# Ordering one chunk's squares, casts and row splits behind the expert blocks they run beside

## The chip, the cores and the metric

One core of one Trainium2 chip runs the whole program. The metric is device time in microseconds (us) from launch to end, as the median of several executions. One further execution was taken with the hardware profiler, and all rows below are of that one.

## The reference

The input is x, 8 sequences of 3584 tokens with 192 channels. First comes a causal convolution of 7 taps along each sequence (8 heads of 24 channels, the taps a softmax of `weight`). Its 28672 rows then go through a mixture of 8 experts: each row is divided by its norm, multiplied with 8 normalised expert embeddings, and sent to the one expert with the largest logit.

```python
out = np.einsum('hk,bskhg->bshg', w, x_unf)          # convolution
xn = x / (np.linalg.norm(x, axis=-1, keepdims=True) + 1e-06)
logits = xn @ en.T / tau
expert_idx = np.argmax(logits, axis=1)
h = np.maximum(x[mask] @ w1[e], 0.0)                 # 192 -> 1024
out[mask] = gate_w[mask, None] * (h @ w2[e])         # 1024 -> 192
```

## The kernel before, in words

**Chunks.** The tokens are cut into 16 chunks of 1792 rows, each laid out as 112 partitions by 16 row groups. For a chunk, `mix` (line 399) does the convolution as 8 matmuls (407) that ScalarE copies back (412), then the 16 sums of squares: three of four on ScalarE (419), one of four on VectorE (422). Both engines write the squares, of which only the sums are wanted, into one tile name, `sq`, with two buffers. `route` (442) then takes the chunk in four groups of four: VectorE multiplies a group by a power of two (451), ScalarE casts it to 16 bits into `rows` (453), and VectorE subtracts the cast from the value to get the low part, in two pieces (455, 458). I call a group's four instructions a split. Transposing DMAs on SyncE's queue (`turn`, 586) bring the split rows to TensorE, which forms the logits (490); VectorE ranks them (509 to 564); and GpSimd's indirect DMAs (593) scatter the rows, with their token numbers, into one list per expert in device memory. `rows` has two buffers, so the casts of chunk c write where the scatters of chunk c-2 read.

**Blocks.** `expert` (748) takes 512, 256 or 128 rows of one expert's list as a block. Its hidden part is 8, 4 or 2 groups of matmuls (770); each fills one PSUM bank of a ring of five. Of each group ScalarE makes the high half of the hidden values (774) and VectorE, after it, the low half (776). The out part (793) reads both halves, for 128 rows at a time, 24 matmuls each; ScalarE scales the result (798) and GpSimd scatters it to the output (800). VectorE also copies the next expert's weights (697, 700) and swaps halves of the input (737).

**Stages.** In the first 150 us the weights are prepared (`prep_weights`, 288), and the first chunks are mixed and routed. Then blocks begin, and the work of the remaining chunks (3 in part, 4 to 15 in full) is emitted beside them, until about 865 us. The rest is blocks alone.

**What sets the order.** `run` (900) emits a block step by step; a step is one hidden group with its two halves, or one 128 rows of the out part. After each step it adds what VectorE and ScalarE have free in such a step to an account (`due`, never over `CAP` = 6 us) and then emits work of chunks as long as neither account is below zero. A split is booked at 0.9 + 0.95 us of VectorE and 0.85 us of ScalarE. While the chunk work waits for something (a `_Gate`), the account fills up. This emission fixes the text of the program. The order on each engine is then chosen at build time by a list scheduler, which runs a model of the machine and gives a free engine the earliest emitted instruction that is ready in the model. SyncE's order alone is the emission's. A dependency without a semaphore, which `_dep(..., False)` writes, makes the scheduler keep two instructions of an engine in order; it costs no instruction. Three such exist already: `behind` puts convolution and logit matmuls behind the last matmul emitted, `under` puts the ranking, the weight copy and the swap behind the last low half emitted (`self.low`), and the scatters name `self.step`, the last high half or output scaling emitted.

Of the kernel before, what the change touches and what calls it, by code (L numbers as in the profile page):

```python
# [13 lines left out]
F32 = mybir.dt.float32  # L14
BF16 = mybir.dt.bfloat16
I32 = mybir.dt.int32
AF = mybir.ActivationFunctionType
ALU = mybir.AluOpType
# [7 lines left out]
D = 192  # L26
# [3 lines left out]
TP = 112  # L30
# [36 lines left out]
def _dep(tc, frm, to, sync=True):  # L67
    cls = mybir.DependencyClass.Sync if sync else mybir.DependencyClass.NoSync
    tc.add_manual_dep(
        frm, to, mybir.DependencyInfo(cls, mybir.DependencyReason.DATA),  # L70
        reason="routed rows are written before they are read",
    )


class _Moe:
# [42 lines left out]
    def ps(self, ring, shape, dt, name):  # L118
        n = 2048 // (2 if dt == F16 else 4)
        t = self.rings[ring].tile([128, n], dt, tag=ring, name=name)  # L120
        w = int(np.prod(shape[1:]))
        v = t[: shape[0], :w]
        if len(shape) == 3:
            v = v.rearrange("p (a b) -> p a b", b=shape[2])
        elif len(shape) == 4:
            v = v.rearrange("p (a b c) -> p a b c", b=shape[2], c=shape[3])
        return v


    def rsqrt(self, n2, shape, name):  # L130
# [157 lines left out]
    def prep_weights(self, e, st):  # L288
        nc = self.nc
        img = self.res[:, e * RES:(e + 1) * RES]  # L290


        st, sw = st
        sr, sv = (v.bitcast(BF16).rearrange("p (n k) -> p n k", k=2)[:, :, 1]
                  for v in (st, sw))
        acc = self.sp.tile([128, 2], F32, tag="w_acc", name="w_acc")
        for k, cols in enumerate(
                ([(sr, 128, i) for i in range(NFC)]
                 + [(sr, 64, i) for i in range(NFC, 2 * NFC)],
                 [(sv, 128, i) for i in range(NFC * D // 128)])):  # L300
            if k and e >= BEHIND:

                i = nc.scalar.activation(
                    out=img[:, W2:W2 + NFC * D], in_=sw, func=AF.Square,
                    accum_out=acc[:, k:k + 1]).ins
                _dep(self.tc, i, self.act[1].name, False)
                yield
                continue
            tr = self.ps("h", [128, 128], F32, "tr_ps")
            for n, (v, rows, i) in enumerate(cols):  # L310
                v = v[0:rows, i * 128:(i + 1) * 128]
                i = nc.tensor.matmul(out=tr, lhsT=v, rhs=v, start=(n == 0),
                                     stop=(n == len(cols) - 1)).ins
                if e >= BEHIND:
                    _dep(self.tc, i, self.turned.name, False)
            dg = self.sp.tile([128, D], F32, tag="sq", name="w_dg")[:, 0:128]
            nc.vector.scalar_tensor_tensor(
                out=dg, in0=tr, scalar=1.0, in1=self.idf, op0=ALU.mult,
                op1=ALU.mult, accum_out=acc[:, k:k + 1])
            yield  # L320
        ps = self.ps("h", [128, 2], F32, "n2_ps")
        nc.tensor.matmul(out=ps, lhsT=self.onef, rhs=acc, start=True, stop=True)
        s, si = self.pow2(ps, [128, 2], 198, "w_p")
        s1, s2 = s[:, 0:1], s[:, 1:2]
        nc.vector.tensor_tensor(out=img[:, WS:WS + 2].bitcast(F32), in0=si[:, 0:1],
                                in1=si[:, 1:2], op=ALU.mult)
        yield
        xb = img[:, 2 * F:W2]
        b = img[:, W2:WS].rearrange("p (c d) -> p c d", d=2 * D)
        s_b = sw.rearrange("p (c d) -> p c d", d=D)  # L330
        hi = [nc.scalar.activation(out=o, in_=i, func=AF.Copy, scale=m).ins
              for o, i, m in ((img[:, 0:F], st[:, 0:F], s1),
                              (xb[0:64, :], st[0:64, F:2 * F], s1[0:64]),
                              (b[:, :, 0:D], s_b, s2))]
        lo = [nc.vector.scalar_tensor_tensor(
            out=o, in0=i, scalar=m, in1=h, op0=ALU.mult, op1=ALU.subtract).ins
              for o, i, m, h in (
                  (img[:, F:2 * F], st[:, 0:F], s1, img[:, 0:F]),
                  (xb[64:128, :], st[0:64, F:2 * F], s1[0:64], xb[0:64, :]),
                  (b[:, :, D:], s_b, s2, b[:, :, 0:D]))]  # L340
        if e >= BEHIND - 1:
            for i in hi:
                _dep(self.tc, i, self.act[e >= BEHIND].name, False)
        for i in lo:
            if e >= BEHIND - 2:
                _dep(self.tc, i, self.dve[e >= BEHIND].name, False)
            elif e:
                _dep(self.tc, i, self.cut.name, False)
        yield
# [36 lines left out]
            _dep(self.tc, i, self.mm.name, False)  # L386


    def under(self, i):
        if self.gated and self.low is not None:  # L390
            _dep(self.tc, i, self.low.name, False)
# [7 lines left out]
    def mix(self, c, ring, first):  # L399
        nc, sp = self.nc, self.sp  # L400

        yield _Gate(self.asked[c] + LAND_X)
        xt = self.xts[c]
        xc = xt[0:TP]
        for h in range(H):
            ps = self.ps(ring, [TP, NT, G], F32, "conv_ps")
            i = nc.tensor.matmul(out=ps, lhsT=self.band[:, h, :],  # L407
                                 rhs=xt[:, :, h * G:(h + 1) * G],
                                 start=True, stop=True).ins
            self.behind(i)  # L410
            self.clk += STEPC
            nc.scalar.copy(out=xc[:, :, h * G:(h + 1) * G], in_=ps)  # L412
            yield 0.0, 0.46

        n2 = sp.tile([TP, NT], F32, tag="n2", name="n2")
        for t in range(NT):
            sq = sp.tile([128, D], F32, tag="sq", name="sq")[0:TP, :]
            if t % 4 < NACT:
                nc.scalar.activation(out=sq, in_=xc[:, t, :], func=AF.Square,  # L419
                                     accum_out=n2[:, t:t + 1])  # L420
            else:
                nc.vector.scalar_tensor_tensor(  # L422
                    out=sq, in0=xc[:, t, :], scalar=1.0, in1=xc[:, t, :],
                    op0=ALU.mult, op1=ALU.mult, accum_out=n2[:, t:t + 1])
            if t % 2:
                yield ((0.54, 0.0), (0.27, 0.35), (0.0, 0.7))[
                    (t % 4 < NACT) + ((t - 1) % 4 < NACT)]
        s, si = self.pow2(n2[:], [TP, NT], 195, "x_p")
        y = self.rsqrt(n2[:], [TP, NT], "x_r")
        f = sp.tile([TP, NT], F32, tag="f", name="f")  # L430
        nc.vector.tensor_tensor(out=f, in0=n2, in1=y, op=ALU.mult)
        nc.vector.scalar_tensor_tensor(out=f, in0=f, scalar=1e-6, in1=s,
                                       op0=ALU.add, op1=ALU.mult)
        nc.vector.reciprocal(out=f, in_=f)
        nc.vector.tensor_scalar(out=f, in0=f, scalar1=self.rtau[:, 0:1],
                                scalar2=None, op0=ALU.mult)

        yield 1.5, 0.0
        self.mixed[c] = xc, s, si, f


    def route(self, c, xbar):
        xTs = []
        nc, sp = self.nc, self.sp
        xc, s, si, f = self.mixed.pop(c)
        r32 = self.rows[c % 2]
        rows = r32[:].bitcast(F16)
        for g in range(0, NT, GX):
            u = slice(g, g + GX)
            sb = s[:, u].unsqueeze(2).to_broadcast([TP, GX, D])  # L450
            nc.vector.tensor_tensor(out=xc[:, u, :], in0=xc[:, u, :], in1=sb,  # L451
                                    op=ALU.mult)
            nc.scalar.copy(out=rows[:, u, 0:D], in_=xc[:, u, :])  # L453
            yield 0.9, 0.85
            nc.vector.tensor_tensor(  # L455
                out=rows[:, u, 256:384], in0=xc[:, u, 0:128],
                in1=rows[:, u, 0:128], op=ALU.subtract)
            self.cut = nc.vector.tensor_tensor(
                out=rows[:, u, 192:256], in0=xc[:, u, 128:192],
                in1=rows[:, u, 128:192], op=ALU.subtract).ins  # L460
            yield 0.95, 0.0
            if xbar and 0 < g <= 2 * GX:
                xTs.append((self.turn(rows, g - GX, GX), self.queue(TURN)))
# [7 lines left out]
        for g in range(NT // GX):  # L471
            if xbar:
                if len(xTs) == g:
                    xTs.append((self.turn(rows, g * GX, GX), self.queue(TURN)))
                xT, at = xTs[g]
                yield _Gate(at + LAND_T)
            else:
                xT = self.xtp.tile([128, GX, 3, TP], F16, tag="xT", name="xT")
                for k in range(3):
                    tp = self.ps("r", [128, GX, TP], F16, "tr_ps")  # L480
                    for a in range(GX):
                        self.turned = nc.tensor.transpose(
                            out=tp[:, a, :],
                            in_=rows[:, g * GX + a, k * 128:(k + 1) * 128],
# [3 lines left out]
            for a in range(GX):  # L488
                for k in range(3):
                    i = nc.tensor.matmul(  # L490
                        out=lg[:, g * GX + a, :], lhsT=xT[:, a, k, :],
# [13 lines left out]
        if self.gated and self.step is not None:  # L505
# [19 lines left out]
                                op=ALU.mult)  # L525
# [462 lines left out]
```

## Time and profile before

| | us |
|---|---|
| median of 3 runs | 1360.71 (1360.64 to 1365.02) |
| the profiled execution | 1354.13 |
| its span, first to last instruction | 1352.4 |
| TensorE busy, mean granted clock | 1190.4 (88%), 0.94 |
| VectorE, ScalarE, GpSimd busy | 834.7, 580.9, 544.1 |

Busy time of TensorE is that of pipelined matmuls. A granted clock of 1.00 is 2.4 GHz and one of 0.50 is 1.2 GHz. A row of waits names the engine and line that sat idle and what ended the wait; "issue" is idle time for which the profile shows no releaser.

### The profile page before, as it was taken

How to read it: one execution, taken by the hardware profiler on the slowest of the kernel's cores; microseconds unless marked ns; L12 is line 12 of the kernel's file. 1: busy time of each engine (PE TensorE's matmuls, PEld its weight loads, DVE VectorE, ACT ScalarE, POOL GpSimd, SP SyncE). 2: the span in 40 equal slices, each digit the busy share in tenths (PEclk: the TensorE clock that was granted, in tenths of full speed). 3: DMA queues.
4: the chain of work that ended last, by engine and by line, in shares of the span. 5: the costliest groups of instructions: out<-in, count | busy, mean ns of one | idle time of the engine just before them, and what ended most of it. 6: DMA issues, size and time to landing. Idle time of an engine off the chain costs nothing. (4 is left out here: it accounts for less than half of the span.)

```text
span 1352.4 us, 28951 instructions
## 1 busy us (share of the span) xinstructions
PE 1190.4 (88%) x10572; PEld 909.4 (67%) x10572; DVE 834.7 (62%) x2218; ACT 580.9 (43%) x1343; POOL 544.1 (40%) x552
## 2 busy tenths in 40 slices
PE   4673789988889998999888999689999999999998
PEld 2542578777776676867556667367767777799787
DVE  3968647677766756676576664454455565467475
ACT  3967343444534644444444633223333333333332
POOL 0064252455544546445445555652222222223232
PEclk9666788899999998999989999899999999999999
DMA  8464524446446354555457444222212122113120
GB/s 247 141 215 113 108 69 99 126 99 135 100 123 149 95 117 112 121 133 129 102 124 152 86 104 96 78 72 51 51 36 55 39 52 46 34 43 66 32 46 23
DMA packets 273952, 129.12 MB, mean 95 GB/s; under 512 B 215774, under 2 KB 264285, under 8 KB 273808
## 3 DMA queue, kind: packets, MB, share of 16 engines
q1 hardware_dynamic: 250000, 80.39, 28.0%
q0 software_dynamic: 23808, 46.87, 11.6%
q8 instruction: 83, 1.36, 0.4%
q14 instruction: 61, 0.50, 0.1%
HBM read 38.35 MB, written 47.53 MB: 64 GB/s over the span
## 5 line engine op out<-in xcount | busy, mean ns | idle before, releaser
L793 PE MATMUL o_ps<-slot,hid 128*128 128x192 f16 x5544 | 514.2, 250 | 60.3 <-issue 26.5
L793 PEld LDWEIGHTS <-hid 128*128 128x128 f16 x5544 | 464.8, 99 | 110.3 <-issue 49.8
L770 PE MATMUL h_ps<-e_xT,slot 128*128 128x256 f16 (+2 forms) x2944 | 506.4, 305 | 26.5 <-issue 15.6
L770 PEld LDWEIGHTS <-slot 128*128 128x128 f16 x3680 | 327.6, 100 | 219.5 <-issue 48.9
L800 POOL DMA_INDIRECT out_dram<-y,e_mt x231 | 258.5, 1119 | 506.9 <-ACT y L798 453.9
L776 DVE SCALAR_TENSOR_TENSOR hid<-h_ps,hid 128x512 f16<-128x512 f32 x462 | 309.6, 686 | 189.0 <-ACT hid L774 159.0
L774 ACT ACTIVATE hid<-h_ps 128x512 f16<-128x512 f32 x462 | 265.4, 598 | 220.8 <-PE h_ps L770 160.4
L593 POOL DMA_INDIRECT rows_d<-rows,di x256 | 267.9, 1046 | 225.0 <-issue 83.7
L798 ACT ACTIVATE y<-o_ps,g 128x192 f32<-128x192 f32 x231 | 95.2, 419 | 334.4 <-PE o_ps L793 255.4
L770 PE MATMUL h_ps<-e_xf,slot 128*128 128x256 f16 (+2 forms) x736 | 212.4, 304 | 1.0 <-issue 1.0
L700 DVE COPY slot<-res 128x3074 f16 x88 | 85.3, 969 | 168.7 <-PE o_ps L793 110.4
L407 PE MATMUL conv_ps<-xt,band 128*112 128x384 f32 x256 | 111.6, 544 | 19.9 <-ACT xt L412 8.6
L453 ACT CAST rows<-xt 112x768 f16<-112x768 f32 x64 | 52.9, 830 | 101.4 <-DMA rows_d<-rows,di 56.7
L412 ACT COPY xt<-conv_ps 112x384 f32<-112x384 f32 x128 | 60.0, 479 | 71.6 <-PE conv_ps L407 54.1
L697 DVE COPY slot<-res 128x3072 f16 x88 | 83.8, 952 | 0.0
L490 PEld LDWEIGHTS <-xT 128*112 128x112 f16 x768 | 57.9, 148 | 28.5 <-DMA xT<-rows 16.3
L455 DVE TENSOR_TENSOR rows<-xt,rows 112x512 f16<-112x512 f32 x64 | 44.0, 687 | 48.2 <-ACT rows L453 37.1
L490 PE MATMUL lg_ps<-ma,xT 128*112 128x16 f16 x512 | 57.2, 204 | 16.7 <-DMA xT<-rows 14.8
L407 PEld LDWEIGHTS conv_ps<-xt,band 128*112 128x112 f32 x256 | 43.2, 195 | 41.7 <-issue 17.9
L419 ACT ACTIVATE sq<-xt 112x192 f32<-112x192 f32 x192 | 67.8, 355 | 2.9 <-DVE sq L422 1.7
L451 DVE TENSOR_TENSOR xt<-xt,x_p_s 112x768 f32<-112x768 f32 x64 | 58.4, 952 | 0.2
L490 PE MATMUL lg_ps<-mb,xT 128*112 128x16 f16 x256 | 46.8, 206 | 1.5 <-ACT xT L486 1.5
(163 smaller groups left out, 531.0 us busy)
## 6 DMA issues: line engine op xcount, KB each, us to landing
xt<-in_dram SPq DMA_DIRECT2D x39, 384.0 KB
xt<-in_dram SPq DMA_DIRECT2D x3, 1440.0 KB
rows_d<-rows,di POOLq DMA_INDIRECT x256
res<-in_dram SPq DMA_DIRECT2D x5, 768.0 KB
out_dram<-y,e_mt POOLq DMA_INDIRECT x231
xT<-rows SPq DMA_TRANSPOSE x224
xt<-in_dram SPq DMA_DIRECT2D x2, 1536.0 KB
hid<-in_dram SPq DMA_DIRECT2D x3, 768.0 KB
```

Of the source, the lines that this page charges most:

```text
L407: i = nc.tensor.matmul(out=ps, lhsT=self.band[:, h, :], rhs=xt[:, :, h * G:(h + 1) * G], start=True, stop=True).ins
L419: nc.scalar.activation(out=sq, in_=xc[:, t, :], func=AF.Square, accum_out=n2[:, t:t + 1])
L490: i = nc.tensor.matmul(out=lg[:, g * GX + a, :], lhsT=xT[:, a, k, :], rhs=self.mb if k == 1 else self.ma, start=(k == 0), stop=(k == 2)).ins
L593: i = self.nc.gpsimd.indirect_dma_start(out=self.rows_d[:, :], out_offset=bass.IndirectOffsetOnAxis(ap=idx, axis=0), in_=src, in_offset=No ...
L697: self.under(nc.vector.tensor_copy(out=self.slot[:, 0:W2], in_=v).ins)
L700: self.nc.vector.tensor_copy(out=self.slot[:, W2:], in_=self.res[:, bass.ds(self.we + W2, RES - W2)])
L770: self.mm = nc.tensor.matmul(out=ps[:, c, :], lhsT=w1(o, b + c), rhs=xk[k], start=(i == 0), stop=(i == 4)).ins
L774: self.step = nc.scalar.activation(out=hh[:, b:b + m, :], in_=ps, func=AF.Relu).ins
L776: self.low = nc.vector.scalar_tensor_tensor(out=hl[:, b:b + m, :], in0=ps, scalar=0.0, in1=hh[:, b:b + m, :], op0=ALU.max, op1=ALU.subtrac ...
L793: self.mm = nc.tensor.matmul(out=o, lhsT=h[:, c, q], rhs=w2[:, c, k:k + D], start=(c + i == 0), stop=(c == NFC - 1 and i == 2)).ins
L798: self.step = nc.scalar.activation(out=y, in_=o, func=AF.Copy, scale=g[:, a:a + 1]).ins
L800: i = nc.gpsimd.indirect_dma_start(out=self.out[:, :], out_offset=bass.IndirectOffsetOnAxis(ap=mt[:, a, 0:1], axis=0), in_=y, in_offset=No ...
```

## The change

Once blocks run (`gated`), the change gives an order without a semaphore to every square, multiply, cast and split part: those of ScalarE go behind `self.step`, those of VectorE behind `self.low`, as they stand at the point of emission. The squares of VectorE, and a throw-away product of the weight preparation, no longer write `sq` but a tile of their own with one buffer, which they share by its tag with `ge` of `select`, a VectorE tile. Instructions, their sizes and the emission stay the same.

```diff
+    def waste(self, p, n):
+        return self.lp.tile([128, D], F32, tag="sl_ge", name="waste")[0:p, 0:n]
...
+    def beside(self, i, act=False):
+        at = self.step if act else self.low
+        if self.gated and at is not None:
+            _dep(self.tc, i, at.name, False)
...
             if t % 4 < NACT:
-                nc.scalar.activation(out=sq, in_=xc[:, t, :], func=AF.Square,
-                                     accum_out=n2[:, t:t + 1])
+                sq = sp.tile([128, D], F32, tag="sq", name="sq")[0:TP, :]
+                self.beside(nc.scalar.activation(
+                    out=sq, in_=xc[:, t, :], func=AF.Square,
+                    accum_out=n2[:, t:t + 1]).ins, True)
             else:
-                nc.vector.scalar_tensor_tensor(
-                    out=sq, in0=xc[:, t, :], scalar=1.0, in1=xc[:, t, :],
-                    op0=ALU.mult, op1=ALU.mult, accum_out=n2[:, t:t + 1])
+                self.beside(nc.vector.scalar_tensor_tensor(
+                    out=self.waste(TP, D), in0=xc[:, t, :], scalar=1.0,
+                    in1=xc[:, t, :], op0=ALU.mult, op1=ALU.mult,
+                    accum_out=n2[:, t:t + 1]).ins)
...
-            nc.vector.tensor_tensor(out=xc[:, u, :], in0=xc[:, u, :], in1=sb,
-                                    op=ALU.mult)
-            nc.scalar.copy(out=rows[:, u, 0:D], in_=xc[:, u, :])
+            self.beside(nc.vector.tensor_tensor(
+                out=xc[:, u, :], in0=xc[:, u, :], in1=sb, op=ALU.mult).ins)
+            self.beside(nc.scalar.copy(
+                out=rows[:, u, 0:D], in_=xc[:, u, :]).ins, True)
             yield 0.9, 0.85
-            nc.vector.tensor_tensor(
+            self.beside(nc.vector.tensor_tensor(
                 out=rows[:, u, 256:384], in0=xc[:, u, 0:128],
-                in1=rows[:, u, 0:128], op=ALU.subtract)
+                in1=rows[:, u, 0:128], op=ALU.subtract).ins)
```

The second piece of the low part (458) gets no order of its own; it is emitted right behind the first and needs the same cast.

## Rows read from the trace of the kernel before

**Rows 1.** Busy time by stretch: start:end, length, engines' busy us (instructions), PEclk, DMA, GB/s.
```profile
200.00:864.00 664.00, 603.80 (x5217) 456.06 (x5216) 442.09 (x1291) 295.28 (x754) 335.60 (x336) 0.97 0.51 115
880.00:1352.00 472.00, 455.56 (x4463) 359.73 (x4461) 258.42 (x477) 168.95 (x321) 133.91 (x124) 1.00 0.20 46
```

**Rows 2.** TensorE's waits, 200 to 864 us: who waited for whom: total, times, longest.
```profile
PE o_ps L793 <- DVE hid L776: 15.5, 19, 2.1
PE o_ps L793 <- issue: 15.0, 33, 1.2
...
PE o_ps L793 <- ACT hid L774: 7.1, 8, 2.0
PE h_ps L770 <- ACT y L798: 2.6, 2, 1.9
PE o_ps L793 <- DVE rows L458: 1.8, 1, 1.8
```

**Rows 3.** Groups of instructions by line, whole span: busy us, mean ns | idle before.
```profile
L776 DVE SCALAR_TENSOR_TENSOR hid<-h_ps,hid 128x512 f16<-128x512 f32 x462 | 309.6, 686 | 189.0 <-ACT hid L774 159.0 <-issue 26.4 <-ACT sq L419 2.0
...
L407 PE MATMUL conv_ps<-xt,band 128*112 128x384 f32 x256 | 111.6, 544 | 19.9 <-ACT xt L412 8.6 <-DMA xt<-in_dram 6.5 <-issue 2.7
...
L451 DVE TENSOR_TENSOR xt<-xt,x_p_s 112x768 f32<-112x768 f32 x64 | 58.4, 952 | 0.2
...
L453 ACT CAST rows<-xt 112x768 f16<-112x768 f32 x64 | 52.9, 830 | 101.4 <-DMA rows_d<-rows,di 56.7 <-issue 25.9 <-DVE xt L451 5.6
L455 DVE TENSOR_TENSOR rows<-xt,rows 112x512 f16<-112x512 f32 x64 | 44.0, 687 | 48.2 <-ACT rows L453 37.1 <-issue 4.3 <-DMA rows_d<-rows,di 4.1
...
L458 DVE TENSOR_TENSOR rows<-xt,rows 112x256 f16<-112x256 f32 x64 | 26.7, 417 | 0.0
```

**Rows 4.** ScalarE's and VectorE's waits, 200 to 864 us.
```profile
ACT rows L453 <- DMA rows_d<-rows,di: 56.7, 19, 7.1
...
DVE rows L455 <- ACT rows L453: 37.1, 16, 4.4
DVE sq L422 <- ACT sq L419: 23.8, 16, 6.2
```

**Rows 5.** Timeline, 381 to 389 us: start us, us, engine, line, what [idle before].
```profile
386.57 0.83 ACT L453 CAST rows<-xt 112x768 f16<-112x768 f32 x1 [5.40 <-DMA rows_d<-rows,di]
...
387.44 0.69 DVE L455 TENSOR_TENSOR rows<-xt,rows 112x512 f16<-112x512 f32 x1 [3.02 <-ACT rows L453]
...
387.96 0.50 PE L793 MATMUL o_ps<-slot,hid 128*128 128x192 f16 x4 [2.04 <-ACT hid L774]
```

**Rows 6.** Chain that ended last, 836 to 860 us: start us, us, what.
```profile
840.88 8.65 PE h_ps L770 x40
849.53 3.14 PE o_ps L793 x38
```

**Rows 7.** Timeline, 362 to 371.5 us, VectorE and TensorE.
```profile
362.06 0.69 DVE L776 SCALAR_TENSOR_TENSOR hid<-h_ps,hid 128x512 f16<-128x512 f32 x1 [0.98 <-ACT sq L419]
...
369.95 0.69 DVE L776 SCALAR_TENSOR_TENSOR hid<-h_ps,hid 128x512 f16<-128x512 f32 x1
...
370.69 1.00 PE L793 MATMUL o_ps<-slot,hid 128*128 128x192 f16 x10 [1.76 <-DVE g L785]
```

**Rows 8.** Timeline, 575.5 to 580.4 us.
```profile
576.75 2.68 DVE L451 TENSOR_TENSOR xt<-xt,x_p_s 112x768 f32<-112x768 f32 x3
...
580.18 0.42 PE L793 MATMUL o_ps<-slot,hid 128*128 128x192 f16 x3 [2.12 <-DVE hid L776]
```

**Rows 9.** Busy time by stretch, with the granted clock (columns as rows 1).
```profile
207.60:214.40 6.80, 6.05 (x41) 5.37 (x39) 5.96 (x16) 0.00 (x0) 0.25 (x1) 0.50 0.27 73
388.50:392.00 3.50, 2.88 (x16) 2.32 (x17) 3.42 (x8) 0.84 (x2) 1.32 (x1) 0.51 0.78 154
```

**Rows 10.** Timeline, 14 to 30 us, VectorE and TensorE.
```profile
25.42 0.91 PE L312 MATMUL tr_ps<-res 128*128 128x128 bf16 x12
...
26.62 0.29 DVE L317 SCALAR_TENSOR_TENSOR w_dg<-tr_ps,idf 128x128 f32<-128x128 f32 x1 [11.82 <-ACT sq L419]
```

More of the change, by code (lines that the diff above doesn't have):

```diff
@@ L315, in prep_weights @@
                     _dep(self.tc, i, self.turned.name, False)
-            dg = self.sp.tile([128, D], F32, tag="sq", name="w_dg")[:, 0:128]
             nc.vector.scalar_tensor_tensor(
-                out=dg, in0=tr, scalar=1.0, in1=self.idf, op0=ALU.mult,
+                out=self.waste(128, 128), in0=tr, scalar=1.0, in1=self.idf, op0=ALU.mult,
                 op1=ALU.mult, accum_out=acc[:, k:k + 1])
@@ L416, in mix @@
         for t in range(NT):
-            sq = sp.tile([128, D], F32, tag="sq", name="sq")[0:TP, :]
             if t % 4 < NACT:
-                nc.scalar.activation(out=sq, in_=xc[:, t, :], func=AF.Square,
-                                     accum_out=n2[:, t:t + 1])
-            else:
-                nc.vector.scalar_tensor_tensor(
-                    out=sq, in0=xc[:, t, :], scalar=1.0, in1=xc[:, t, :],
-                    op0=ALU.mult, op1=ALU.mult, accum_out=n2[:, t:t + 1])
+                sq = sp.tile([128, D], F32, tag="sq", name="sq")[0:TP, :]
+                self.beside(nc.scalar.activation(
+                    out=sq, in_=xc[:, t, :], func=AF.Square,
+                    accum_out=n2[:, t:t + 1]).ins, True)
+            else:
+                self.beside(nc.vector.scalar_tensor_tensor(
+                    out=self.waste(TP, D), in0=xc[:, t, :], scalar=1.0,
+                    in1=xc[:, t, :], op0=ALU.mult, op1=ALU.mult,
+                    accum_out=n2[:, t:t + 1]).ins)
             if t % 2:
```

## The prediction

> **What bounds the kernel now.** I read the busy time by stretch first. While blocks run alone, TensorE is busy for all but 16 of 472 us; in the stage in which chunk work runs beside blocks it is idle for 60 of 664 us, and VectorE, at 442 us, is at 67% [rows 1]. So TensorE sets the pace, and the change can touch only the 60 us, the clock, and what it adds to them. The waits of TensorE in that stage say who ended them [rows 2]: the low half 15.5, the high half 7.1, the output scaling 2.6 and a split part 1.8 us, 27.0 together. The rows marked "issue" name no releaser; I leave them as they are. I went through the gaps behind the 27 us one by one: in about 25 us of them a multiply, a cast or a split part ran on VectorE or ScalarE within 2 us ahead.
>
> Why splits stand there is seen in two places. At 386.6 us a cast of ScalarE has waited 5.4 us for a scatter of the chunk that used the same `rows` buffer; VectorE's split part waits 3.0 us for the cast, the low half stands behind that, and TensorE is idle for 2.0 us [rows 5]. Such waits of casts are 56.7 us in the stage, in 19 pieces, and those of split parts for casts 37.1 us [rows 4]. At 576.8 us three multiplies run in a row ahead of a low half, and TensorE waits 2.1 us [rows 8]. Both come from one habit: the list scheduler pulls splits forward into what its model thinks idle. I numbered the program's instructions as the code emits them and read the engines' queues against it. In the gated stage all 50 multiplies stand 1 to 21 low halves ahead of their place, and 45 of 50 casts are ahead of theirs. No square is ahead: they wait for the last convolution copy anyway.
>
> **The change, part by part.** *The squares' orders* bind nothing, since no square is ahead: 0 us, hidden by the convolutions that feed them. *The tile of its own* takes away VectorE's waits for ScalarE's squares, 23.8 us in the stage [rows 4]. In the gaps that I went through next to nothing had a square ahead and a low half as releaser, so TensorE gets nothing: 0. In the head the same sharing shows a wait of 11.8 us, which could be worth anything from 0 to 11.8; but the matmuls whose product that instruction reads ended at 26.3 us, 0.3 us before it began [rows 10], so I take 0.3, since both rows belong to the very wait. The head may also come out in another order; nothing bounds that, and I leave it at 0.
>
> *The splits' orders* are the change. They take away what pulling forward costs: up to 27.0, and I take 25. A split issues no DMA, but transposes, loads of x and scatters wait for it. SyncE keeps the order of emission, and the planner emits a chunk's logits at least 5.1 + 4.5 us of its own clock (`TURN`, `LAND_T`) after the transposes; the latest bunch below ends 8.2 us after its place, so the lead covers it. The casts come at a place where the scatters of chunk c-2 have all been emitted (`route` starts with at most 16 pending), so most of the 56.7 us goes, and with it the 37.1.
>
> What do they add? The account of the planner fills to 6 us while a chunk waits for a gate, and a split books 1.85 us, so three or four splits are then emitted at one place. An order behind the last low half is also a licence: the splits are older than the next low half, all four multiplies are ready, and the scheduler gives a free engine the oldest ready instruction. So they should run as one bunch ahead of the next low half. A split takes VectorE 0.952 + 0.687 + 0.417 = 2.06 us [rows 3], four take 8.2. ScalarE's four casts, 0.83 us each [rows 3], lie beside that; a high half behind a cast is late by less than VectorE is, and costs nothing of its own.
>
> The trace of before has no such bunch in a hidden part, so its price is bounded. From below it is 0: a stretch of 7.2 us without a low half that begins in an out part, with four hidden groups to come, costs TensorE 1.8 us [rows 7]. From above it is 0.8 of the bunch, as where three multiplies meet a TensorE that has already run out of other work: 2.12 of 2.68 us [rows 8]. Between them I count what TensorE still has to do before it needs the last held half: a hidden group takes 8.65 / 8 = 1.08 us, and the out part reaches half number 8 after 7 x 3 matmuls of 3.14 / 38 us, 1.75 us in all [rows 6]; each further half takes 0.69 us [rows 3]. With j groups still to come the price is bunch + 0.69 (j - 1) - 1.08 j - 1.75. Stepping the planner through the code gives the places of the 12 full chunks:
> - Five late in a hidden part. Chunk 8, after 7 of 8 groups: 8.2 - 1.08 - 1.75 = 5.4. Chunks 11 and 12, after 6: 5.0 each. Chunk 15, after 5: 4.6. Chunk 5, three splits (6.2) after 2 of 4 groups, where the last half is needed after 1.5 us: 3.2. Together 23.
> - Four in an out part (4, 7, 10, 14): as in [rows 7], 1.8 each, 7.
> - Two beside eight convolutions (6, 13), 0.44 us each of TensorE [rows 3], which cover them: 1. One spread over three groups (9): 1.
>
> That is 32 us; the ends I keep are 0 and 51 (the five at 0.8 x 8.2 = 6.5, the rest doubled).
>
> *The clock.* After such waits the granted clock falls to half: 6.8 us at 1.2 GHz after the wait at 205 us, 3.5 us after that at 388 us [rows 9]; two more of these lengths follow split waits, so 20.6 us at half clock lose some 8 us beside what was idle anyway. These go. After the change eight waits of 2 to 5 us would bring one each, at 1.75 to 3.4 us; I take 2, so 16. Net + 8, with ends of - 8 and + 19.
>
> Sum: - 25 + 32 + 8 - 0.3 = + 15 us on the profiled execution's 1354.1 (its span is 1352.4), so 1369. That execution lies 6.6 us under the median of the three runs, 1360.7; I add them: **1376 us**.
>
> **The rivals.** *The places of emission are good ones: faster.* The emission was paced by what each step leaves free, and five PSUM banks let TensorE run on. If low halves slip in between multiplies while a cast is awaited, or the bunches mostly fall where rows 7's price or less holds, 25 us and 8 us of clock go and some 3 to 10 come: 1361 - 23 to 30, or 1331 to 1338. For it speaks that the ranking, which is under the same kind of order, costs TensorE little now; against it, that the ranking is a chain in which each instruction waits for the one before and lets a low half through, while multiplies wait for nothing. It decides above about 2.5 us a chunk: below that the forecast turns. 0.33.
>
> *No change.* Gains and bunches cancel within 7 us, or order on an engine that is a third idle matters to nobody: about 1361. 0.13. The Trainium skill, in "Perfetto Trace Analysis" under "Identifying the Most-Contended Engine", says to find the engine with the highest occupancy and work on that one first; by that VectorE, at 67%, would not be the place and the sum would be 0. The 15.5 us of TensorE's waits on low halves [rows 2] speak against reading it so here: what is late is an instruction, not an engine.
>
> *Slower by another way.* The split rows come too late for the transposes, these hold the queue of SyncE, and TensorE meets its logit matmuls, which stand in its own queue, before the transposed rows have landed. If each of 12 chunks lost the bunch beyond the covered 6 us, 2.2 us, twice, that is some 50 us less the 33 saved: about 1380. 0.06. The forecast itself gets 0.48.
>
> **How the numbers follow.** A measurement of this kernel tells some 0.5% (6.8 us) from no change. Faster 0.33, same 0.13, slower 0.48 + 0.06 = 0.54. The forecast's own range is 1362 to 1406: from a bunch price cut by a third with half the clock term, to 51 and + 19. The 8-in-10 range must hold most of the faster case too: 1329 to 1406.
>
> **What would show each step.** Right: the 56.7 us of casts waiting for scatters nearly gone, and VectorE's waits for ScalarE's squares too; three or four multiplies between two low halves late in a hidden part, five times; TensorE's waits on the low half up from 15.5 to about 35 us, in pieces of 3 to 6; eight stretches at half clock instead of four. Wrong: low halves between the multiplies of a bunch, or pieces of TensorE idle time under 2 us there; then the faster case holds. TensorE waiting for transposed rows for more than a few us would be the third rival. A first block that starts more than 3 us earlier or later would be a step that I left at 0.

## The result, and the profile after

The changed kernel takes 1381.88 us (median of four executions, 1379.47 to 1384.68), the kernel before 1362.2 us beside it: a ratio of 1.0143, 95% interval 1.0112 to 1.0173. It is slower by 20 us, where 1376 was forecast. That agreement hides that the terms of the sum were wrong, and on the two other chips on which the changed kernel ran the sign was the opposite one. The profiled execution of the changed kernel is one of the four, 1384.68 us with a span of 1383.0; before it was 1354.13 with 1352.4. So the spans of the two traces differ by 30.6 us where the medians differ by 19.7: some 11 us of what follows lie between executions and not between the kernels. The lines of the code have moved: high half 786, low half 788, output matmul 805, multiply 462, cast 464, split parts 467 and 470, transposes 601.

From the page of the changed kernel, busy time of the engines and TensorE's granted clock in 40 slices:

```profile
PE 1208.0 (87%) x10572; PEld 921.2 (67%) x10572; DVE 839.5 (61%) x2218; ACT 581.0 (42%) x1343; POOL 538.6 (39%) x552
...
PEclk9555789897899998999989999999999999999999
```

The same 10572 matmuls kept TensorE busy for 1190.4 us before; the other 17.6 us are a lower clock. The span grew by 30.6, so idle time grew by 13.0. By releaser, that is 35 us more of "issue" less 22 of other waits: 16 less between the first block and the last routing, 8 less in the head, 2 more behind (the first block starts at 147 to 148 us in both).

Busy time by stretch of the changed kernel (columns as [rows 1]):

```profile
200.00:864.00 664.00, 590.04 (x5015) 448.28 (x5014) 432.50 (x1234) 291.19 (x741) 312.46 (x319) 0.93 0.49 111
...
880.00:1352.00 472.00, 449.62 (x4269) 346.81 (x4267) 253.19 (x511) 163.98 (x313) 144.80 (x137) 0.98 0.21 49
```

Against [rows 1], 202 matmuls fewer are done in the first stretch and its clock is 0.93 instead of 0.97. The second stretch starts with chunk work still running.

TensorE's waits in the changed kernel, 200 to 890 us (total, times, longest):

```profile
PE o_ps L805 <- issue: 35.4, 44, 2.3
PE lg_ps L502 <- issue: 13.3, 17, 2.1
PE h_ps L782 <- issue: 9.6, 17, 1.1
PE h_ps L782 <- DVE hid L788: 4.9, 2, 4.1
PE o_ps L805 <- DVE hid L788: 4.6, 8, 1.2
PE o_ps L805 <- ACT hid L786: 3.7, 3, 2.3
PE lg_ps L502 <- DMA xT<-rows: 1.9, 2, 1.0
```

and the "issue" rows of the kernel before in the same stretch:

```profile
PE h_ps L770 <- issue: 16.6, 22, 6.3
PE o_ps L793 <- issue: 15.0, 33, 1.2
```

This is the opposite of the forecast. Waits with a releaser on VectorE or ScalarE shrink, as the orders were to make them [rows 2]. What grows is "issue", idle time for which the profile shows no releaser: 58.3 us in the three rows of the changed kernel, 31.6 in the two of before.

What the casts and squares waited for is gone. Groups by line, whole span, of the changed kernel (compare [rows 3]):

```profile
L462 DVE TENSOR_TENSOR xt<-xt,x_p_s 112x768 f32<-112x768 f32 x64 | 58.0, 951 | 0.0
L464 ACT CAST rows<-xt 112x768 f16<-112x768 f32 x64 | 51.9, 832 | 8.8 <-DVE xt L462 7.2 <-issue 0.6 <-DVE rows L470 0.5
L467 DVE TENSOR_TENSOR rows<-xt,rows 112x512 f16<-112x512 f32 x64 | 43.8, 685 | 0.4
```

Casts idled 101.4 us before, 8.8 now; the first split part 48.2, now 0.4.

The bunches are there too, and of the forecast length: three times all four splits of a chunk stand between two low halves. Timeline of the changed kernel, 561 to 573.7 us:

```profile
561.94 0.69 DVE L788 SCALAR_TENSOR_TENSOR hid<-h_ps,hid 128x512 f16<-128x512 f32 x1 [0.40 <-ACT hid L786]
...
563.75 3.59 DVE L462 TENSOR_TENSOR xt<-xt,x_p_s 112x768 f32<-112x768 f32 x4
...
565.07 1.47 PE L416 MATMUL conv_ps<-xt,band 128*112 128x384 f32 x4
...
566.38 1.91 PE L782 MATMUL h_ps<-e_xT,slot 128*128 128x256 f16 x16
...
570.19 0.60 PE L782 MATMUL h_ps<-e_xT,slot 128*128 128x256 f16 x4
...
572.67 0.42 DVE L470 TENSOR_TENSOR rows<-xt,rows 112x256 f16<-112x256 f32 x1
...
573.00 0.68 DVE L788 SCALAR_TENSOR_TENSOR hid<-h_ps,hid 128x512 f16<-128x512 f32 x1
```

Between the low halves at 561.94 and 573.00 stand four multiplies and their eight split parts, 8.0 us, and TensorE does not idle at all in that time (busy for 11.06 of 11.06 us): it has outputs, convolutions and the hidden groups of the next block to do. The low half at 561.94 is the last of its block, the one at 573.00 the first of the next.

Last, the lulls, as I call stretches in which TensorE and ScalarE, and mostly VectorE, all but stop though the profile shows nothing that they wait for. Two nearly equal stretches of the changed kernel, the first in a lull, the second just ahead of it (columns as [rows 1]):

```profile
697.40:708.50 11.10, 1.88 (x10) 0.81 (x9) 0.31 (x2) 0.00 (x0) 6.54 (x7) 0.70 0.51 134
685.00:696.00 11.00, 11.00 (x69) 5.88 (x68) 9.77 (x44) 7.29 (x23) 4.95 (x6) 1.00 0.49 123
```

and from the timeline inside it:

```profile
701.12 0.32 PE L805 MATMUL o_ps<-slot,hid 128*128 128x192 f16 x2 [1.32 <-issue]
701.14 0.94 POOL L605 DMA_INDIRECT rows_d<-rows,di  x1 [0.30 <-issue]
...
702.38 0.93 POOL L605 DMA_INDIRECT rows_d<-rows,di  x1 [0.30 <-issue]
703.28 0.32 PE L805 MATMUL o_ps<-slot,hid 128*128 128x192 f16 x1 [1.84 <-issue]
...
704.70 0.32 PE L805 MATMUL o_ps<-slot,hid 128*128 128x192 f16 x1 [1.11 <-issue]
```

TensorE does 10 matmuls in 11 us instead of 69, VectorE two small instructions; GpSimd goes on with its scatters, one each 1.24 us. The clock falls to half in the lull, at 701.9 us, and stays there for 10.2. I count as issue idle every gap of TensorE over 0.15 us in the whole span that the profile puts to issue: 46.8 us before, 82.1 after. From 150 us on it is 43.3 and 74.7; where expectations below give 47 and 82 us from there on, these are the sums of the whole span.

### The profile page after: what moved, and what is told of

Its sections match the earlier page's. It is cut to its first block, busy times and chain, and to the rows that moved or that the text cites. A ratio compares the mean times of both kernels' runs of the same rounds, so it can differ in the third digit from the quotient of the medians.

```text
span 1383.0 us, 28928 instructions
## 1 busy us (share of the span) xinstructions
PE 1208.0 (87%) x10572; PEld 921.2 (67%) x10572; DVE 839.5 (61%) x2218; ACT 581.0 (42%) x1343; POOL 538.6 (39%) x552
## 4 chain that ended last, share of the span: by engine, by line
PE 36%; issue 34%; POOL 12%; DVE 5%; ACT 2%; DMA 2%; another core or an unknown queue 2%; SPq 2%; POOLq 1%; DVEq 0%; ACTq 0%
PE h_ps L782 14%; PE o_ps L805 14%; POOL out_dram L812 8%; PE conv_ps L416 4%; POOL rows_d L605 4%; PE lg_ps L502 2%; SPq L601 2%; DVE hid L788 1%; DMA xT<-rows 1%; DVE rows L467 1%; DVE xt L462 1%; ACT hid L786 1%; ACT sq L428 1%; ACT res L334 0%
## 5 line engine op out<-in xcount | busy, mean ns | idle before, releaser
L805 PE MATMUL o_ps<-slot,hid 128*128 128x192 f16 x5544 | 523.2, 251 | 60.3 <-issue 42.0
L805 PEld LDWEIGHTS <-hid 128*128 128x128 f16 x5544 | 470.4, 100 | 114.9 <-issue 66.4
L782 PE MATMUL h_ps<-e_xT,slot 128*128 128x256 f16 (+2 forms) x2944 | 512.3, 307 | 22.7 <-issue 10.0
L605 POOL DMA_INDIRECT rows_d<-rows,di x256 | 259.2, 1013 | 170.4 <-issue 93.7
L416 PE MATMUL conv_ps<-xt,band 128*112 128x384 f32 x256 | 114.6, 557 | 24.6 <-issue 9.2
L502 PEld LDWEIGHTS <-xT 128*112 128x112 f16 x768 | 66.5, 152 | 49.1 <-issue 19.2
L502 PE MATMUL lg_ps<-ma,xT 128*112 128x16 f16 x512 | 64.7, 204 | 26.5 <-DMA xT<-rows 14.9
L749 DVE COPY e_xf<-e_xT 64x256 f16<-64x256 f16 (+2 forms) x184 | 44.4, 241 | 8.9 <-DMA e_xT<-rows_d 4.0
```

Source lines behind the costliest of these rows:

```text
L416: i = nc.tensor.matmul(out=ps, lhsT=self.band[:, h, :], rhs=xt[:, :, h * G:(h + 1) * G], start=True, stop=True).ins
L502: i = nc.tensor.matmul(out=lg[:, g * GX + a, :], lhsT=xT[:, a, k, :], rhs=self.mb if k == 1 else self.ma, start=(k == 0), stop=(k == 2)).ins
L605: i = self.nc.gpsimd.indirect_dma_start(out=self.rows_d[:, :], out_offset=bass.IndirectOffsetOnAxis(ap=idx, axis=0), in_=src, in_offset=No ...
L782: self.mm = nc.tensor.matmul(out=ps[:, c, :], lhsT=w1(o, b + c), rhs=xk[k], start=(i == 0), stop=(i == 4)).ins
L805: self.mm = nc.tensor.matmul(out=o, lhsT=h[:, c, q], rhs=w2[:, c, k:k + D], start=(c + i == 0), stop=(c == NFC - 1 and i == 2)).ins
```

## The experiments

Two theories stood at first. BUNCH was the prediction's: the orders on the splits make low halves late. SCATTER: the lulls belong to long unbroken runs of GpSimd's scatters, and the change makes those. After seven runs I formed a third, RELIEF: the orders take waits off TensorE, and DMA is late next. Each group of runs below was on one chip, with the kernel before beside it; before had 1271.92, 1269.66, 1270.85 and, in the last group, 1365.53 us.

**The tile alone** (e1): VectorE's squares write to `waste`, no order is added.

```diff
     def beside(self, i, act=False):
-        at = self.step if act else self.low
-        if self.gated and at is not None:
-            _dep(self.tc, i, at.name, False)
+        return
```

> Two theories. BUNCH: the rise of 20 us comes from the orders of the row splits, which let multiplies and subtracts pile up ahead of a low half. SCATTER: the rise comes from GpSimd's row scatters falling into longer unbroken runs; TensorE issues one instruction per 0.7 us late in such a run without any wait shown, and drops to half clock. This kernel has VectorE's own tile for the squares and no new order. BUNCH: 1362 us, within 5 (as the prediction's price of 0.3). SCATTER: within 5 of 1362 if TensorE's idle put to issue stays near the 39 us of the kernel before; any rise comes with a rise of that.

Measured 1282.0 us, ratio 1.0094 (1.0066 to 1.0122): slower by 10 us, where both theories and the prediction expected no change. Its trace has no lull at all (issue idle 2.7 us), and TensorE's waits for ScalarE's output scaling are 10.7 us. Timeline of this kernel, 242 to 246.5 us (line 462 is here the cast, 808 the output scaling):

```profile
242.50 0.68 DVE L465 TENSOR_TENSOR rows<-xt,rows 112x512 f16<-112x512 f32 x1
...
244.74 0.83 ACT L462 CAST rows<-xt 112x768 f16<-112x768 f32 x1 [6.08 <-DMA rows_d<-rows,di]
245.48 0.73 ACT L808 ACTIVATE y<-o_ps,g 128x192 f32<-128x192 f32 x2
...
245.94 0.60 PE L780 MATMUL h_ps<-e_xT,slot 128*128 128x256 f16 x4 [3.74 <-ACT y L808]
```

A cast stands 6 us at the head of ScalarE's queue until a scatter has read its buffer; two finished outputs stand behind it, and TensorE has no free bank. The casts' waits for DMAs are 124.6 us in this kernel between 140 and 810 us, against 100.0 in the kernel before on such a chip (e6). That the scheduler found more room to pull casts forward, with the squares out of each other's way, is my inference; no run tests it.

**Tile and the squares' orders** (e2): the changed kernel without `beside` on multiply, cast and first split part.

```diff
...
-            self.beside(nc.scalar.copy(
-                out=rows[:, u, 0:D], in_=xc[:, u, :]).ins, True)
...
+            nc.scalar.copy(out=rows[:, u, 0:D], in_=xc[:, u, :])
...
```

> Own tile and the squares' orders, the row splits free as before. BUNCH: 1362 us within 5, bunches of multiplies no longer than before, casts still wait some 50 us for scatters. SCATTER: no size of its own; the time goes with the issue idle (39 us before, 73 us after) and with half-clock time (44 us before, some 93 us after).

1280.14 us, 1.0072 (1.0048 to 1.0095). The interval overlaps that of e1, so the squares' orders cost nothing that shows; the tile's price stays. Issue idle 2.9 us.

**The splits' orders alone** (e3): the kernel before plus `beside` on lines 451, 453 and 455.

```diff
...
-            nc.scalar.copy(out=rows[:, u, 0:D], in_=xc[:, u, :])
...
+            self.beside(nc.scalar.copy(
+                out=rows[:, u, 0:D], in_=xc[:, u, :]).ins, True)
...
```

> Orders on the splits' multiplies, casts and first subtracts alone; squares and their tile as before. BUNCH: all of the rise, 1376 to 1386 us, with bunches of 8 to 12 split pieces. SCATTER: a rise only with more issue idle than 39 us. If tile, squares and splits each stay under 1368, the rise belongs to none of them alone but to how the order of the scatters falls out.

1258.43 us, 0.9896 (0.9863 to 0.9928): faster. BUNCH falls here, with bunches of up to 12 pieces in the trace as in the changed kernel.

**Spare scatters** (e4): the kernel before with 78 further scatters of the same shape to a scratch tensor, behind the chunks.

```diff
...
+        i = nc.gpsimd.indirect_dma_start(
+            out=self.junk[:, :],
...
+            in_=self.rows[0][:, 0, :], in_offset=None).ins
...
+        _dep(tc, i, self.step.name)
...
```

Their order behind `self.step` has a semaphore, and so has that of the program's own scatters; they are not, as was said ahead, a third case of an order without one.

> The kernel before with extra scatters of finished rows to a scratch tensor, late in the program where no chunk is mixed any more: one at every hidden step of twelve blocks (runs of 9 and more with the outputs' scatters), then at every fourth hidden step of twelve blocks (runs of 1 to 6). It leaves nothing out. BUNCH: no more than 5 us over before (GpSimd has room there, TensorE is 100% busy), or, where outputs wait for GpSimd, waits that the trace names. SCATTER: in the first twelve blocks TensorE idles 1 to 4 us per block put to issue, followed by half clock, 20 to 60 us in all; in the second twelve under 3 us in all.

1277.42 us, 1.0057 (1.0037 to 1.0078), issue idle 3.2 us. Between 938 and 1060 us stand five unbroken runs of 11 to 18 scatters, and no lull. The 5 us lie behind the last matmul: the span ends 12.0 us after it, in the trace of before on such a chip (e6) 6.4. SCATTER is out as a rule; at most it describes chips that have lulls.

**The changed kernel and the one before, unaltered, and the shared tile** (e5, e6, e7). In e7 all orders stay and the squares share the old ring:

```diff
...
-                    out=self.waste(TP, D), in0=xc[:, t, :], scalar=1.0,
+                    out=sq, in0=xc[:, t, :], scalar=1.0,
...
```

> The changed kernel, unaltered, on a chip where TensorE's idle put to issue was under 4 us in four kernels (it was 47 us before and 82 us after in the first two traces, from 150 us on). If the lulls made the rise: no slower than before here, about the sum of its parts, 1.0094 x 0.9896 = 0.999 of before. BUNCH: still 1.010 to 1.018 of before, with low halves late behind split pieces. SCATTER by a run's length alone is already out, since runs of 10 and more had no lull in those four.

> The kernel before, unaltered, for a trace on the same chip: issue idle under 4 us, waits of TensorE in the mixed stage on a low half some 20 us and on ScalarE some 15 us, as the spare scatters' kernel showed them up to 790 us.

> The changed kernel with the squares of both engines in the ring of two as before, all orders kept. If the own tile alone costs (1.0094 when alone), this is 0.985 to 0.995 of before and faster than the changed kernel by about 1%. BUNCH gives the tile no price: the same time as the changed kernel within 0.4%.

The changed kernel took 1261.66 us, 0.9924 (0.9895 to 0.9953): the sign turns. With the shared tile 1258.41, 0.9911 (0.9876 to 0.9946), so beside the orders the tile costs nothing that shows, and not the 1% that I had expected. TensorE's waits of the kernel before on this chip, 140 to 810 us:

```profile
PE o_ps L793 <- DVE hid L776: 17.8, 21, 3.8
PE o_ps L793 <- ACT hid L774: 11.4, 7, 3.6
PE h_ps L770 <- DVE hid L776: 3.8, 3, 2.9
PE conv_ps L407 <- ACT xt L412: 3.7, 2, 2.3
PE h_ps L770 <- ACT y L798: 1.8, 2, 1.5
PE o_ps L793 <- DVE slot L700: 0.4, 1, 0.4
```

and of the changed kernel in the same stretch:

```profile
PE lg_ps L502 <- DMA xT<-rows: 16.9, 26, 1.8
PE h_ps L782 <- DMA e_xT<-rows_d: 8.9, 5, 3.0
PE o_ps L805 <- DVE hid L788: 3.4, 6, 1.2
PE conv_ps L416 <- DMA xt<-in_dram: 3.1, 2, 2.0
PE conv_ps L416 <- ACT xt L421: 1.2, 1, 1.2
```

No row is put to issue. The six waits on VectorE and ScalarE, 38.9 us, have shrunk to 4.6, and 28.9 us of waits on DMA stand there: the routing matmuls wait for the transposed rows. (3.0 of the 28.9 end with the start of the first block, at 142 us here; in the kernel before that is at 137 us, outside the stretch.) What these wait for stands in SyncE's waits of the changed kernel, same stretch:

```profile
SPq L601 <- DVE rows L470: 141.2, 12, 22.2
```

Once per chunk a transpose holds SyncE's queue until the last split part is written; in the trace of the first pair that row is 185.3 us in 12 pieces. So the third rival's mechanism is at work, for 17 us of TensorE's waits and not 50.

**The orders of one engine** (e8, e9), **a later routing** (e10), and the changed kernel once more (e11). e8 has `beside` on the cast alone, e9 on the multiply and the first split part; e10 is e3 with

```diff
-LAND_X, LAND_T = 9.0, 4.5
+LAND_X, LAND_T = 9.0, 6.0
```

> The kernel before with ScalarE's casts ordered behind the block's latest eviction, nothing else. RELIEF (the orders take waits off TensorE, and DMA is late next): where TensorE has no lulls, the casts' 86 us of waits on scatters go, and with them TensorE's 11 us on ScalarE's halves; 0.993 to 0.997 of before. BUNCH: 1.000, as casts are not on VectorE.

> The kernel before with the multiplies and the first subtracts ordered behind the latest low half, the casts free. RELIEF: TensorE's waits on low halves fall from 24 us to under 12, ScalarE's stay; 0.993 to 0.998 of before. BUNCH: slower than before, 1.005 to 1.015, with low halves late behind the split pieces.

> The splits' orders alone (0.9896 of before) with the time that the program allows a transpose to land, LAND_T, raised from 4.5 to 6.0 us, so that the routing matmuls are emitted one to two steps later. RELIEF: TensorE's 17 us of waits for transposes in the routing matmuls fall under 7, and the time to 0.980 to 0.988 of before. If those waits were hidden, or come back elsewhere: 0.988 to 0.992.

> The changed kernel again, as the measure beside the three others. Without lulls 0.990 to 0.996 of before, with issue idle under 4 us; on a chip with lulls (over 40 us of issue idle from 150 us on) 1.011 to 1.018. If its time exceeds before's without lulls, the lulls are not what turned the sign.

e8 took 1233.09 us, 0.9715 (0.9689 to 0.9741), a far larger gain than expected; e9 1258.52, 0.9902 (0.9863 to 0.9941), more of a gain than either theory had, with 7.3 us of waits on low halves, so BUNCH is out here too; e10 1241.93, 0.9786 (0.9759 to 0.9814), just under RELIEF's range; e11 1260.8, 0.9934 (0.9913 to 0.9955). TensorE's waits with the casts' order alone, 140 to 810 us:

```profile
PE lg_ps L497 <- DMA xT<-rows: 6.3, 7, 1.9
PE o_ps L800 <- DVE hid L783: 4.6, 6, 1.3
PE h_ps L777 <- DVE hid L783: 3.6, 2, 2.8
PE h_ps L777 <- DMA e_xT<-rows_d: 1.7, 1, 1.7
```

The casts' order takes away most of what all the orders together do: the 86.2 us of casts waiting for scatters that the kernel before has in that stretch (e6) are gone, and the waits for low halves, many of which stood behind split parts that waited for casts, fall from 21.6 us to 8.2; the 11.4 us for high halves are gone. TensorE's busy time over the whole span is 1144.1 us against 1157.2 in e6, for the same matmuls. VectorE's orders alone also free the casts, since a cast reads what the multiply writes: their waits for scatters in e9 are

```profile
ACT rows L459 <- DMA rows_d<-rows,di: 2.4, 2, 1.3
```

but TensorE waits 20.6 us for transposes there. e3 adds VectorE's orders to e8 and is 25 us slower (1258.43 against 1233.09, on two chips whose kernel before differs by 1 us). Its waits for transposes are 17.0 us instead of 6.3, those for fetches 5.8 instead of 1.7, and TensorE's clock falls to half four times between the first block and the end, which with the casts alone it never does. e10 gives the transposes more time and halves their row to 8.7; the kernel before and the casts' order alone were not run with the later routing on such a chip. That is the price of VectorE's orders: not paid at the low half, but by SyncE's transposes behind the split parts. The time for which a transpose holds SyncE's queue does not tell that price by itself. In e8 it is nearly as long,

```profile
SPq L596 <- DVE rows L465: 119.2, 12, 16.9
```

and TensorE waits 6.3 us; the 22 us more of the changed kernel come with 10.6 more of TensorE's waits.

The runs side by side, all on chips without lulls:

| what is ordered or changed | ratio to before |
|---|---|
| own tile (e1) | 1.0094 |
| own tile, squares (e2) | 1.0072 |
| multiplies and first split parts (e9) | 0.9902 |
| casts (e8) | 0.9715 |
| multiplies, casts, first split parts (e3) | 0.9896 |
| the same, routing later (e10) | 0.9786 |
| the same and squares, shared tile (e7) | 0.9911 |
| all of the change (e5, e11) | 0.9924, 0.9934 |

**Casts alone with the later routing** (e12), to beat both kernels.

> ScalarE's casts ordered (0.9715 of before) and LAND_T at 6.0 us. RELIEF: TensorE's 6 us of waits for transposes fall under 3 and nothing takes their place: 0.965 to 0.971 of before without lulls. If the later routing makes chunks and their blocks late instead: 0.972 to 0.980. On a chip with lulls both scale with what the lulls do; the ratio there has no forecast, its issue idle would tell.

This run fell on a chip like that of the first pair: before 1365.53 us. There it took 1369.8, 1.0033 (1.0004 to 1.0062): no gain. TensorE's waits, 200 to 890 us:

```profile
PE o_ps L800 <- issue: 35.3, 41, 2.3
PE h_ps L777 <- issue: 18.4, 25, 1.4
PE lg_ps L497 <- issue: 5.8, 10, 1.0
PE o_ps L800 <- DVE hid L783: 3.3, 3, 1.3
```

Issue idle is 76.4 us, near the changed kernel's 82.1, with none of VectorE's orders and no tile. So on such a chip the casts' order, with the later routing, seems enough to bring the larger lulls, as far as one trace of each kernel tells; before was timed on this chip and not traced, and its 46.8 us are from the first pair. Which of the two does it, and how the casts' order alone fares there, was not run.

## Why the prediction was right in sign and wrong in its terms

The number came out near by luck. The largest price of the sum, 32 us at low halves, measured 2.5, and what stood in for it, 35 us of "issue", had no term.

- *Squares' orders at 0*: right (e2 against e1).
- *The tile at 0*: right beside the other orders (e7 against e5), wrong alone, where it costs 10 us. I had looked for squares among the last instructions ahead of a gap; what the wait for ScalarE's squares did, as far as e1's trace tells, was to keep VectorE from running on to multiplies, and the casts behind them from standing earlier in ScalarE's queue. That was not tested.
- *The splits' orders take 25 of 27 us off TensorE*: right in the mechanism, and too large on the first pair. The 27.0 of [rows 2] are 13.2 in the changed kernel, 14 less; 38.9 became 4.6 on the second chip. The 56.7 us of [rows 4] went. One reading under it was wrong: at 388 us [rows 5] TensorE waits for the high half, by the row's own releaser, and not for the low half. The high half stood behind the waiting cast on ScalarE, which is what e8 takes away.
- *Bunches cost 32 us at low halves*: this step failed. The bunches came, but in the nine largest (seven pieces or more) TensorE idles 2.5 us in all. I had put five of them late in a hidden part, where a block's outputs need the held low halves. In the trace all nine stand behind the last low half of a block and ahead of the first of the next, as at 561.94: the older block's halves went first, for a reason that no run shows, and TensorE had outputs, convolutions and the next block's groups to do. The faster rival named this case. (The two bunches beside convolutions were priced with 0.44 us a convolution; [rows 3] has 256 records for 16 chunks of 8, so one is two records and 0.87 us.)
- *The transposes' lead covers the bunch*: failed on the chips without lulls. In e5 16.9 us of TensorE's waits are for transposes, in 26 pieces. The rival's chance of 0.06 was too low and its price, 50 us, too high; VectorE's orders cost 25 us over the casts' order.
- *Clock at +8*: mis-sized on the first pair, where busy time rose by 17.6. Half-clock stretches as [rows 9] now followed the lulls, 16 of 18 between 150 us and the last matmuls, and not the low halves.
- *The issue rows left as they are*: by the account of the two traces, this is what made the change a loss. They carried no price in my sum, and they grew by 35 us; with 17.6 of clock and 22 less of other waits that is the 30.6 by which the span grew. Where lulls don't occur, the same change gains 8 to 10 us, the faster rival's sign at a third of its 23 to 30 us; with the routing later, and without the squares' part, it gains 29 (e10).

The rule of the Trainium skill, "Perfetto Trace Analysis", "Identifying the Most-Contended Engine", to optimize the engine with the highest occupancy first, does not by itself say whose instructions to change. TensorE has the highest in e6 (91% by its matmuls, 71% by its weight loads; VectorE 66%), and the largest gain, 38 us, came from ordering 64 casts on ScalarE, which is busy for 46% of that span.

Open is why some chips have lulls, and why there both tightened kernels have more of them. The runs show that the rise comes together with the lulls, not what makes them.

## What to carry to other kernels

When a scheduler pulls an instruction forward, ask first whether it can stand waiting at the head of its engine's queue: ordering the one that waits (the cast for its scatter) was worth 38 us, while ordering the ones that never wait was worth 12 alone (e9) and took 25 away on top of it (e3), with the DMAs behind them late. A gain of 1% should be measured on several chips, with "issue" idle and the granted clock read beside it, because here the sign depended on the chip.

## What the hardware showed unexpectedly

The same kernel took 1362 to 1366 us in the first pair and beside e12, and 1270 to 1272 on three other chips, at the same mean duration of the low half, 0.686 us. The record names no chip that was visited twice, so the runs do not tell the chip from what was particular to it at that time. On the slower ones TensorE and ScalarE, and mostly VectorE, all but stop for 2 to 13 us at a time while GpSimd goes on issuing scatters, in the lull above at 1.24 us each, and TensorE's granted clock goes to half in many of these lulls. On the others, issue idle was 2.6 to 3.2 us in eleven traces, at most 0.4 of it behind 150 us. In the three traces with lulls more than half of it stands in GpSimd's unbroken runs of six and more scatters (0.35 us or less between two): 31.2 of 46.8 us before, 53.6 of 82.1 after, 43.0 of 76.4 in e12, though such runs cover only 250 to 265 us. The DMA packets that load instructions do not mark the lulls: of the 18 that last 1.5 us or more in the changed kernel from 150 us on, 14 have none that starts inside. Neither such runs nor 78 added scatters brought any lull on the other chips.
